# Hashed attention and a gated projection on one core: the seams between the stages are rewritten

## Chip, cores and metric

One NeuronCore of a Trainium2 chip runs the whole program in one launch. The metric is the device time of one execution in microseconds (us), the median of several runs. Before the change it is 904.46 us (3 runs, 904.19 to 904.78). The engines are TensorE (PE; its weight loads are shown as PEld), VectorE (DVE), ScalarE (ACT), GpSimd (POOL) and SyncE (SP); SP, ACT and POOL issue DMA transfers.

## The reference

```python
q_bits = (einsum('bhsd,dk->bhsk', q, proj) > 0)          # B,H,S,D = 4,8,768,64; 6 bits
k_bits = (einsum('bhsd,dk->bhsk', k, proj) > 0)
mask   = bucket(q_bits)[:, :, :, None] == bucket(k_bits)[:, :, None, :]
scores = where(mask, q @ k.T / sqrt(D), -1e9)
attn   = softmax(scores);  x = (attn @ v).reshape(B*S, H*D)   # 3072 x 512
h      = x @ w_in                                        # 512 x 2048
g      = h * erf(softplus(h))
out    = g @ w_out                                       # 3072 x 512, float32
```

A query attends only to keys whose six hash bits are the same as its own.

## The kernel before

**Attention.** The 32 heads are taken as 16 pairs; a pair fills the 128 partitions with two heads of 64. `fetch` loads q, k and v of a pair. Until now it issues one DMA for each head of the pair. For pair 0 (`quick`) q and k come in halves, and the first half of k goes by ACT's queue while everything else goes by SP's.

The hash bits of a pair become a second, bf16 operand of the score: a tile `both` with rows that add a huge amount when all bits agree, so that the exponential of a pair that does not agree is 0. Pair 0 and pair 1 make it directly (`hash_bits` with `proj_sb`, 64 columns for a head pair; then Sign on ACT, two weighings and a doubling on DVE: `place_first`, `weigh_first`, `double_first`). From pair 2 on it takes the shorter matmul with `proj_q` (line 845, 32 columns, four in the array at once), Sign (`sign_of`), one weighing (`weigh_bits`), and a way through DRAM that puts the rows in place: `leave_bits` writes them out and `place_bits` reads them back, both on POOL's DMA queue, into a `both` tile that was cleared (`clean`).

A pair has 4 score steps of 3 blocks each (line 557), then 4 weigh steps (line 642). PSUM holds three score blocks. `divisor` (line 687) sums the exponentials over the keys with a matmul against ones, and the reciprocal takes a way over DRAM (`spread`, `gather`, `invert`, `ungather`, `widen`).

Before all that, `WARM` matmuls on a tile of ones (line 807) run while the first loads are on their way. proj is loaded once into `proj_in` on POOL's queue and copied by DVE into `proj_sb` and `proj_q`.

**Bound.** The exponential is taken without a maximum. `measure` collects the squares of q and k; `judge` sums them over the partitions on PE (line 1746) and DVE takes the maxima, the product and the comparison, into `flag`. At the end of the program every engine loads `flag` (line 1776), and if the bound does not hold the general version runs (`tc.If`). With these inputs it does not run.

**Feed-forward.** Both products run as Strassen-like seven-product forms: P1 to P7 (line 1248) and M1 to M7 (line 1361), 24 blocks in all. `combine` makes the outputs of one tile of 512 tokens from the M banks and sends them; of the last tile, step 0 is a copy on ACT, steps 1 to 6 are whole additions on DVE, and steps 7 and 8 add the two halves of bank M3 and send each by ACT's queue.

**Order.** Each engine runs its instructions in written order. That order comes from a planner (`arrange`) that is given for each operation an engine, a guessed cost, what it comes after, and a rank; it runs its own clock and takes the operation that can start first, and between those that can start together the one of lower rank. For operations of rank 0 that are not on PE, a start within `PATIENCE` (0.16) of the first counts as together. An operation is written (its instructions are emitted) in the planner's order. Waits between engines are put in automatically from what each instruction reads and writes, in the order in which it was written.

PE's order in attention is a fixed chain: 4 scores, 4 weighs, then the next bits and the divisor; the bits of pair 1 come after the 4 scores of pair 0. Weight pieces (`fetch_weights`) are issued on POOL from the third on, each after the conversion (`add_rest`) of the third one before it.

Of the kernel before, what the change touches and what calls it, by code (L numbers as in the profile page):

```python
# [54 lines left out]
F32 = mybir.dt.float32  # L55
# [8 lines left out]
P = 128  # L64
# [132 lines left out]
def kernel(  # L197
# [35 lines left out]
    QR = 32  # L233
    QB = QR // 2
    WARM = 10
# [52 lines left out]
    nc.vector.memset(proj_q, 0.0)  # L288
    for ab in range(2):
        rows = slice(ab * D, ab * D + D)  # L290
        nc.vector.tensor_copy(
            out=proj_q[rows, ab * QB : ab * QB + NBIT],
            in_=proj_in[rows, ab * NBIT : (ab + 1) * NBIT],
        )
# [55 lines left out]
    def fetch(i, load, quick=False):  # L350
        d = dict(
            q=load.tile([P, S], F32, name="q", tag="q"),
            k=load.tile([P, S], F32, name="k", tag="k"),
            v=load.tile([P, NC, P], F32, name="v", tag="v"),
        )
        b, j = divmod(i, JP)
        parts = ((0, "q"), (0, "k"), (1, "k"), (1, "q")) if quick else ((None, "q"), (None, "k"))
        for half, what in parts:
            cols = slice(0, S) if half is None else slice(half * HS, half * HS + HS)
            queue = nc.scalar if quick and what == "k" and half == 0 else nc.sync  # L360
            for ab in range(2):
# [58 lines left out]
    def attention():  # L420
        NS = NPAIR * 4
        with (
# [18 lines left out]
            nc.vector.memset(e_even[:, :, :, HS : HS + 1], 1.0)  # L441
            e_odd = area[:, 0 : NE * S].rearrange("p (n a c) -> p n a c", n=NE, a=2)
# [279 lines left out]
            def spread(i):  # L722

                d = pairs[i]
                zd = d["zd"] = dram.tile([2, 4, HS // 2], F32, name="zd", tag="zd")
                d["zc"] = small.tile([P, 2 * S // P], F32, name="zc", tag="zc")
                nc.sync.dma_start(
                    out=zd.rearrange("h n c -> n h c"),
                    in_=d["z"][0 : 3 * QR + 1 : QR, 0:HS].rearrange("n (h c) -> n h c", h=2),
                )  # L730

            def gather(i):
                d = pairs[i]
                nc.sync.dma_start(
                    out=d["zc"],
                    in_=d.pop("zd")
                    .rearrange("h n c -> (h n c)")
                    .rearrange("(p c) -> p c", c=2 * S // P),
                )
# [64 lines left out]
            pairs[0] = fetch(0, load, quick=True)  # L804
            warm = bank("warm")
# [84 lines left out]
            def place_first():  # L890

                cols = slice(0, S)
                sign_bits(pairs[1], lambda what: both[1][:, "qk".index(what[0]), :], cols)

            def weigh_first(ab):
                spread_bits(pairs[1], slice(0, S), ab)

            def double_first():
                double_bits(pairs[1], slice(0, S))

# [19 lines left out]
            for what, n in order:  # L920
                free = slots[-3] if len(slots) >= 3 else ()
                if what == "score":
                    i = n // 4
                    after = (("double_first",) if i == 1 else ("place_bits", i),)
# [4 lines left out]
                elif what == "bits":  # L929
                    pe(bits_of, (n,), 0.80 if n > 1 else 1.44, (("start_pair", n),) + free)  # L930
                    slots.append((("sign_of", n),) if n > 1 else (("place_first",),))
# [54 lines left out]
            for i in range(NPAIR):  # L986
                n = 4 * i
                if i:
# [4 lines left out]
                        3.6,  # L993
# [3 lines left out]
                        late=3.5,  # L997
                    )
                    if i == 1:
                        op(place_first, (), "ACT", 0.9, (0, n - 2, 9), (("bits_of", i),))  # L1000
                        for ab in (1, 0):
                            op(weigh_first, (ab,), "DVE", 0.43, (0, n - 2, 1), (("place_first",),))
                        op(double_first, (), "DVE", 0.35, (0, n - 2, 2), (("weigh_first", 0), ("weigh_first", 1)))
                    else:
                        op(sign_of, (i,), "ACT", 0.6, (0, n - 6, 9), (("bits_of", i), ("leave_bits", i - 1)))
                        op(weigh_bits, (i,), "DVE", 0.33, (0, n - 6, 1), (("sign_of", i),))
                        op(leave_bits, (i,), "POOL", 0.7, (0, n - 6, 2), (("weigh_bits", i),), late=4.0, far=True)
                        op(
                            place_bits,
                            (i,),  # L1010
                            "POOL",
                            1.2,
                            (0, n - 6, 3),
                            (("leave_bits", i), ("score", n - 5, 2), ("clean", i - 2)),
                            late=3.6,
                        )
# [27 lines left out]
            for n in range(2):  # L1044
                op(clean, (n,), "POOL", 1.4, (0, 4 * n), (("score", 4 * n + 3, 2),), late=0.3)
# [155 lines left out]
    def feed_forward(check, late):  # L1201
        again = late is None
        with (
# [503 lines left out]
            if late:  # L1707
# [33 lines left out]
    def judge():  # L1741

        ps = bank("bound")[:, 0 : 4 * NPAIR]
        for ab in range(2):
# [7 lines left out]
            )  # L1752
        for ab in range(2):
# [5 lines left out]
            )  # L1759
        both = norms[:, :, 0, :]  # L1760
# [11 lines left out]

    with tc.manual_schedule():
        late = attention()
        feed_forward(judge, late)
    again = nc.values_load(flag[0:1, 0:1], min_val=0, max_val=1)
    with tc.If(again > 0):
# [55 lines left out]
```

## Time and profile before

| | |
|---|---|
| median of 3 runs | 904.46 us |
| the profiled execution, its time | 904.72 us |
| its span, first to last instruction | 902.9 us |
| PE busy | 894.3 us (99%) |
| DVE, ACT, POOL busy | 668.5, 563.3, 57.9 us |
| first matmul (warm) | 0.99 us |
| first hash matmul | 5.31 us |
| start of the scores of pair 1 | 27.33 us |
| first product of the feed-forward | 313.5 us |
| end of the last matmul | 896.2 us |

The span is what the profiler saw between the first and the last instruction; the execution's own time is 1.8 us longer. A row of the chain of waits is: start, duration, engine, tile, line, count. A row of the timeline is: start, duration, engine, line, operation, output<-inputs, shape, count, and in brackets how long the engine stood idle before it and what ended that. "SPq", "ACTq" are instructions of an engine's sequencer, DMA issues among them. A row of DMA issues is: output<-input, issuing engine, count, KB of each, and the median time from issue to landing. A matmul on float32 appears as two records.

### The profile page before, as it was taken

The page shows a single profiled execution, that of the slowest core. Times are in us where ns is not written, and L with a number is a line of the kernel's source. Part 1 is how long each engine was busy: PE and PEld are TensorE (multiplying, and loading weights), DVE is VectorE, ACT ScalarE, POOL GpSimd, SP SyncE. Part 2 cuts the span into 40 slices and gives each one's busy share as a digit, 9 for nine tenths or more (in the row PEclk, how much of TensorE's full clock was granted, in tenths as well). Part 3 has the DMA queues.
Part 4 walks back from the last instruction along what each step waited for, and adds up shares of the span by engine and source line. Part 5 has one row for each costly group of instructions (what it writes and reads, how often), then busy time and mean ns, then how long its engine had stood idle before and what let it go on. Part 6 is the DMA issues. An engine that isn't in the chain of part 4 may idle for free.

```text
span 902.9 us, 12780 instructions
## 1 busy us (share of the span) xinstructions
PE 894.3 (99%) x5016; PEld 670.9 (74%) x5016; DVE 668.5 (74%) x837; ACT 563.3 (62%) x808; POOL 57.9 (6%) x95
## 2 busy tenths in 40 slices
PE   9999999999999999999999999999999999999997
PEld 5455554455544588888888888888888888888886
DVE  5999999999999879995666556666776666655652
ACT  6788888788886668855645455545655555545520
POOL 1211211111110000000000001000100010000000
PEclk9999999999999999999999999999999999999999
DMA  9547655667551322202231013211421122111211
GB/s 228 149 128 183 200 166 142 196 173 195 154 157 60 101 89 65 82 36 70 59 106 58 14 49 103 82 36 47 105 83 36 36 74 78 35 36 57 63 68 50
DMA packets 65156, 86.82 MB, mean 96 GB/s; under 512 B 34364, under 2 KB 47772, under 8 KB 65088
## 3 DMA queue, kind: packets, MB, share of 16 engines
q1 hardware_dynamic: 56528, 63.81, 24.8%
q0 software_dynamic: 8112, 21.66, 8.6%
q8 instruction: 41, 0.67, 0.3%
q10 hardware_dynamic: 448, 0.46, 0.2%
q14 instruction: 27, 0.22, 0.1%
HBM read 64.67 MB, written 17.30 MB: 91 GB/s over the span
## 4 chain that ended last, share of the span: by engine, by line
PE 99%; DVE 0%; issue 0%; ACT 0%; DVEq 0%
PE M L1361 32%; PE X L1248 29%; PE st L557 17%; PE av L642 14%; PE M L1248 3%; PE bits L845 1%; PE bits L687 1%; PE warm L807 0%; PE bits L377 0%; PE z_ps L687 0%; DVE e L1288 0%; DVE h L1270 0%; ACT both L390 0%; DVE u L1396 0%; DVE norms L1754 0%
## 5 line engine op out<-in xcount | busy, mean ns | idle before, releaser
L1288 DVE SCALAR_TENSOR_TENSOR e<-w,e 128x1024 f32<-128x1024 f32 x144 | 173.7, 1220 | 8.4 <-ACT w L1282 3.9
L1248 PE MATMUL X<-area,w_in_sb 128*128 128x256 f32 x680 | 160.6, 379 | 0.0
L1282 ACT ACTIVATE w<-h,cq 128x1024 f32<-128x1024 f32 x144 | 155.6, 1136 | 0.1
L557 PE MATMUL st<-q,k 64*128 64x384 f32 x768 | 155.1, 482 | 0.0
L1270 DVE TENSOR_TENSOR h<-X,h 128x512 f32<-128x512 f32 x65 | 44.8, 689 | 144.4 <-PE X L1248 144.4
L1248 PEld LDWEIGHTS X<-area,w_in_sb 128*128 128x128 f32 x680 | 129.2, 190 | 17.6
L1361 PE MATMUL M<-w_out_sb,h 128*128 128x256 f32 x576 | 141.1, 379 | 0.0
L1248 PE MATMUL X<-area 128*128 128x256 f32 x520 | 122.8, 379 | 0.0
L1361 PEld LDWEIGHTS M<-w_out_sb,h 128*128 128x128 f32 x576 | 109.4, 190 | 14.9
L1266 ACT COPY h<-X 128x512 f32<-128x512 f32 x85 | 49.3, 580 | 111.4 <-PE X L1248 111.3
L1248 PEld LDWEIGHTS X<-area 128*128 128x128 f32 x520 | 98.8, 190 | 13.4
L1278 ACT ACTIVATE e<-h,cq 128x1024 f32<-128x1024 f32 x48 | 55.1, 1148 | 85.9 <-DVE h L1270 85.8
L1361 PE MATMUL M<-wt,S 128*128 128x256 f32 x384 | 95.1, 379 | 0.0
L557 PEld LDWEIGHTS st<-q,k 64*128 64x128 f32 x768 | 68.8, 187 | 29.7 <-issue 27.2
L630 DVE TENSOR_TENSOR area<-area 128x1536 f32<-128x1536 f32 (+1 forms) x46 | 79.2, 1723 | 7.5 <-ACT area L584 6.3
L1361 PEld LDWEIGHTS M<-wt,S 128*128 128x128 f32 x384 | 73.0, 190 | 9.9
L584 ACT ACTIVATE e_even<-st 128x768 f32<-128x768 f32 x96 | 70.6, 822 | 0.4 <-PE st L557 0.3
L584 ACT ACTIVATE area<-st 128x768 f32<-128x768 f32 x90 | 68.0, 817 | 0.0
L642 PE MATMUL av<-e_even,v 128*64 128x385 f32 x384 | 65.6, 490 | 0.0
L557 PE MATMUL st<-both 64*128 64x384 bf16 x384 | 63.5, 323 | 0.3 <-ACT both L390 0.3
L1303 DVE TENSOR_TENSOR h<-h,e 128x1024 f32<-128x1024 f32 x48 | 57.9, 1220 | 4.6 <-ACT e L1299 4.6
L642 PE MATMUL av<-area,v 128*64 128x384 f32 x360 | 60.6, 486 | 0.0
(129 smaller groups left out, 976.8 us busy)
## 6 DMA issues: line engine op xcount, KB each, us to landing
wt<-wt SPq DMA_DIRECT2D x24, 768.0 KB, 4.2
raw<-in_w_out_dram POOLq DMA_DIRECT2D x16, 512.0 KB, 4.2
raw<-in_w_in_dram POOLq DMA_DIRECT2D x14, 512.0 KB, 4.6
v<-in_v_dram SPq DMA_DIRECT2D x32, 192.0 KB, 4.6
q<-in_qkT_dram SPq DMA_DIRECT2D x30, 192.0 KB, 4.2
k<-in_qkT_dram SPq DMA_DIRECT2D x30, 192.0 KB, 4.7
r<-rd SPq DMA_DIRECT2D x30, 192.0 KB, 3.7
xs<-x SPq DMA_DIRECT2D x15, 384.0 KB, 3.0
```

The source lines that it names most:

```text
L557: nc.tensor.matmul(out=st[:, ab, 0:HS], lhsT=d["k" + src][rows, keys], rhs=d["q" + src][rows, cols], start=(part == 0), stop=(part == 1),)
L584: nc.scalar.activation(out=e[:, :, 0:HS], in_=st[:, :, 0:HS], func=AF.Exp, scale=scale)
L630: nc.vector.tensor_tensor(out=into, in0=one, in1=two, op=ALU.add)
L642: nc.tensor.matmul(out=d["av", half][rows, 0:w], lhsT=d["v"][:, g * GC + c, rows], rhs=e[:, ab, 0:w], start=(g == 0 and c == 0), stop=(g = ...
L1248: nc.tensor.matmul(out=d[where][:, u, :], lhsT=a[:, kc, f : f + P], rhs=b[:, kc, :], start=(first and u == 0 and kc == 0), stop=(last and ...
L1266: nc.scalar.copy(out=quarter(p, q), in_=st[p][where])
L1270: nc.vector.tensor_tensor(out=h, in0=st[p][where], in1=h, op=ALU.add)
L1278: nc.scalar.activation(out=s, in_=unit(p, v), func=AF.Sigmoid, bias=cq[:, n : n + 1])
L1282: nc.scalar.activation(out=q, in_=unit(p, v), func=AF.Sigmoid, scale=GATE_S[j][0], bias=cq[:, j : j + 1])
L1288: nc.vector.scalar_tensor_tensor(out=s, in0=st[p].pop(("q", v, j)), scalar=GATE_S[j][2], in1=s, op0=ALU.add, op1=ALU.mult,)
L1303: nc.vector.tensor_tensor(out=h, in0=h, in1=st[p].pop(("s", v)), op=ALU.mult)
L1361: nc.tensor.matmul(out=banks[name][:, sub, :], lhsT=a[:, u, sub * P : (sub + 1) * P], rhs=b[:, u, :], start=(c == 0 and k == 0), stop=(c = ...
```

## The change

- `fetch` issues one DMA for both heads of q and one for both of k; v stays two. proj is loaded twice without a copy by DVE: `proj_sb` on ACT's queue after the first k, `proj_q` on POOL's queue after the row numbers. `WARM` is 7 instead of 10.
- Pair 1 makes its hash bits the way of the later pairs (short matmul, Sign, one weighing, `leave_bits`, `place_bits`). Its matmul moves from behind the four scores of pair 0 to behind the second of them. `both[1]` is cleared once by DVE at the start, and only `both[0]` by POOL. The planner's cost and delay of `start_pair(1)` become 0.5 and 1.6 instead of 3.6 and 3.5.
- `divisor` does four matmuls of 384 columns instead of eight of 192; `spread` writes four rows.
- The check of the bound is cut into four: `measured` (the matmuls), `judge` (two reductions on DVE), `decide` (the four small operations that end in `flag`, of low rank, so wherever DVE is idle), and `ask` (every engine loads `flag`), written just before step 0 of the last `combine`.
- The last two matmuls of M3 of the last block are held back and written after step 7 of the last `combine`, ahead of step 8.

```diff
-    WARM = 10
+    WARM = 7
...
-    proj_in = const.tile([P, 2 * NBIT], F32, name="proj_in")
-    nc.gpsimd.dma_start(out=proj_in, in_=proj2)
     nc.vector.memset(proj_sb, 0.0)
-    for ab in range(2):
-        rows = slice(ab * D, ab * D + D)
-        nc.vector.tensor_copy(
-            out=proj_sb[rows, ab * QR : ab * QR + NBIT],
-            in_=proj_in[rows, ab * NBIT : (ab + 1) * NBIT],
-        )
+    nc.vector.memset(proj_q, 0.0)
+
+    def load_proj(queue, into):
+
+        queue.dma_start(
+            out=into[:, :].rearrange("p (a n) -> p a n", a=2)[:, :, 0:NBIT],
+            in_=proj2.rearrange("p (a n) -> p a n", a=2),
         )
+
     row = const.tile([P, 1], F32, name="row")
     nc.gpsimd.dma_start(out=row, in_=bucket)
+    load_proj(nc.gpsimd, proj_q)
...
-            for ab in range(2):
-                queue.dma_start(
-                    out=d[what][ab * D : ab * D + D, cols],
-                    in_=qkT[2 * i + ab, "qk".index(what) * D : "qk".index(what) * D + D, cols],
-                )
+            at = "qk".index(what) * D
+            queue.dma_start(
+                out=d[what][:, cols],
+                in_=qkT[2 * i : 2 * i + 2, at : at + D, cols],
+            )
...
             nc.vector.memset(e_even[:, :, :, HS : HS + 1], 1.0)
+            nc.vector.memset(both[1], 0.0)
...
-                for half in range(2):
-                    for n in range(4):
-                        ab, part = divmod(n, 2)
-                        nc.tensor.matmul(
-                            out=z[n * QR : (n + 1) * QR, half * HS // 2 : (half + 1) * HS // 2],
-                            lhsT=ones[:, 0:QR],
-                            rhs=d["sum"][:, half, ab, part * HS // 2 : (part + 1) * HS // 2],
-                            start=True,
-                            stop=True,
-                        )
+                for n in range(4):
+                    half, ab = divmod(n, 2)
+                    nc.tensor.matmul(
+                        out=z[n * QR : (n + 1) * QR, :],
+                        lhsT=ones[:, 0:QR],
+                        rhs=d["sum"][:, half, ab, :],
+                        start=True,
+                        stop=True,
+                    )
...
             pairs[0] = fetch(0, load, quick=True)
+            load_proj(nc.scalar, proj_sb)
...
-                if i == 1:
-                    hash_bits(pairs[i], big)
-                    return
                 d = pairs[i]
...
             for i in range(NPAIR):
-                order += [("score", 4 * i + k) for k in range(4)]
-                if i == 0:
-                    order.append(("bits", 1))
+                for k in range(4):
+                    order.append(("score", 4 * i + k))
+                    if i == 0 and k == 1:
+                        order.append(("bits", 1))
...
-                    after = (("double_first",) if i == 1 else ("place_bits", i),)
+                    after = (("place_bits", i),)
...
-                        3.6,
+                        3.6 if i > 1 else 0.5,
...
-                        late=3.5,
-                    )
+                        late=3.5 if i > 1 else 1.6,
+                    )
...
-            for n in range(2):
-                op(clean, (n,), "POOL", 1.4, (0, 4 * n), (("score", 4 * n + 3, 2),), late=0.3)
+            op(clean, (0,), "POOL", 1.4, (0, 0), (("score", 3, 2),), late=0.3)
...
-                op(("check", 0), "PE", 0.3, (0, 1, 9), check, (), after=(("P3", 0), ("late", 0)), late=1.5)
+                op(("check", 0), "PE", 0.2, (0, 1, 9), check[0], (), after=(("P3", 0), ("late", 0)))
+                op(("check", 1), "DVE", 0.4, (0, 1, 9.5), check[1], (), after=(("check", 0),))
+                op(("check", 2), "DVE", 0.6, (2, 8, 0), check[2], (), after=(("check", 1),))
                 for each in ops:
                     if each.name == ("P2", FILL - 1):
-                        each.after += (("check", 0),)
+                        each.after += (("check", 1),)
...
+            held = {("M3", NP - 1, f): None for f in (2, 3)}
             for each in arrange(ops, dict(h=8, e=4, w=4, wt=2), PATIENCE):
+                if check and each.name == ("combine", NTILE - 1, 0):
+                    check[3]()
+                if each.name in held:
+                    held[each.name] = each
+                    continue
                 each.emit()
+                if each.name == ("combine", NTILE - 1, 7):
+                    for other in held.values():
+                        other.emit()
...
+    def ask():
+
+        bound["again"] = nc.values_load(flag[0:1, 0:1], min_val=0, max_val=1)
+
     with tc.manual_schedule():
         late = attention()
-        feed_forward(judge, late)
-    again = nc.values_load(flag[0:1, 0:1], min_val=0, max_val=1)
-    with tc.If(again > 0):
+        feed_forward((measured, judge, decide, ask), late)
+    with tc.If(bound["again"] > 0):
```

More of the change, by code (lines that the diff above doesn't have):

```diff
@@ L287 @@
     nc.vector.reduce_sum(out=weight[:, 1:2], in_=steps[:, 2:5], axis=AX.X)
-    nc.vector.memset(proj_q, 0.0)
-    for ab in range(2):
[L290 to L293, printed above, removed]
-        )
     nc.vector.reduce_sum(out=weight_q, in_=steps[:, 5:8], axis=AX.X)
@@ L360, in fetch @@
             queue = nc.scalar if quick and what == "k" and half == 0 else nc.sync
-            for ab in range(2):
-                queue.dma_start(
-                    out=d[what][ab * D : ab * D + D, cols],
-                    in_=qkT[2 * i + ab, "qk".index(what) * D : "qk".index(what) * D + D, cols],
-                )
+            at = "qk".index(what) * D
[3 more added lines that the diff above has]
+            )
         for ab in range(2):
@@ L724, in spread @@
                 d = pairs[i]
-                zd = d["zd"] = dram.tile([2, 4, HS // 2], F32, name="zd", tag="zd")
+                zd = d["zd"] = dram.tile([4, HS], F32, name="zd", tag="zd")
                 d["zc"] = small.tile([P, 2 * S // P], F32, name="zc", tag="zc")
-                nc.sync.dma_start(
-                    out=zd.rearrange("h n c -> n h c"),
-                    in_=d["z"][0 : 3 * QR + 1 : QR, 0:HS].rearrange("n (h c) -> n h c", h=2),
-                )
+                nc.sync.dma_start(out=zd, in_=d["z"][0 : 3 * QR + 1 : QR, 0:HS])
             def gather(i):
@@ L736, in gather @@
                     in_=d.pop("zd")
-                    .rearrange("h n c -> (h n c)")
+                    .rearrange("n c -> (n c)")
                     .rearrange("(p c) -> p c", c=2 * S // P),
@@ L888, in place_bits @@
                     )
[L890 to L899, printed above, removed]
             def clean(n):
@@ L929, in attention @@
                 elif what == "bits":
-                    pe(bits_of, (n,), 0.80 if n > 1 else 1.44, (("start_pair", n),) + free)
-                    slots.append((("sign_of", n),) if n > 1 else (("place_first",),))
+                    pe(bits_of, (n,), 0.80, (("start_pair", n),) + free)
+                    slots.append((("sign_of", n),))
                 elif what == "divisor":
@@ L996, in attention @@
                         + tuple(("measure", i - 3, m, half) for m in range(2) for half in range(2)),
-                        late=3.5,
+                        late=3.5 if i > 1 else 1.6,
                     )
[L999 to L1016, printed above, removed]
+                    op(sign_of, (i,), "ACT", 0.6, (0, n - 6, 9), (("bits_of", i), ("leave_bits", i - 1)))
+                    op(weigh_bits, (i,), "DVE", 0.33, (0, n - 6, 1), (("sign_of", i),))
+                    op(leave_bits, (i,), "POOL", 0.7, (0, n - 6, 2), (("weigh_bits", i),), late=4.0, far=True)
+                    op(
+                        place_bits,
+                        (i,),
+                        "POOL",
+                        1.2,
+                        (0, n - 6, 3),
+                        (("leave_bits", i), ("score", n - 5, 2), ("clean", i - 2)),
+                        late=3.6,
+                    )
                 for m in range(2):
@@ L1739, with measured @@
     top = const.tile([1, 1], F32, name="top")
-    def judge():
-        ps = bank("bound")[:, 0 : 4 * NPAIR]
+    bound = {}
+    def measured():
+        ps = bound["ps"] = bank("bound")[:, 0 : 4 * NPAIR]
         for ab in range(2):
@@ L1752, in judge @@
             )
+    def judge():
+        ps = bound["ps"]
         for ab in range(2):
@@ L1759, in judge, with decide @@
             )
+    def decide():
         both = norms[:, :, 0, :]
```

## The prediction

> **What bounds the kernel now.** I read the page first (sections 1 and 4), then the chain of waits over 0–30, 330–345 and 890–903 us, then the timeline, the waits and the DMA issues at those places.
>
> ```profile
> span 902.9 us, 12780 instructions
> PE 894.3 (99%) x5016; PEld 670.9 (74%) x5016; DVE 668.5 (74%) x837; ACT 563.3 (62%) x808; POOL 57.9 (6%) x95
> PE 99%; DVE 0%; issue 0%; ACT 0%; DVEq 0%
> ```
>
> TensorE is the bound. 902.9 - 894.3 leaves 8.6 us without a matmul: 0.99 before the first, 6.69 after the last (ends 896.21), some 0.9 between. So this change can only shorten the seams, or take matmuls away. The chain of waits at the start:
>
> ```profile
> 0.99 4.49 PE warm L807 x20
> 5.48 0.70 PE bits L377 x4
> 9.17 8.25 PE st L557 x60
> 17.42 1.44 PE bits L377 x8
> 18.86 7.75 PE av L642 x48
> 26.62 0.78 PE bits L845 x8
> ```
>
> The warm matmuls are filler (10 calls, two records each). The pair-1 hash at line 377 costs 1.44; the other form, line 845, 0.78. The one mid-kernel stall:
>
> ```profile
> 333.71 0.23 PE bound L1746 x4
> 333.96 0.21 DVE norms L1754
> ...
> 334.44 0.19 DVE norms L1761
> 334.65 0.18 DVE top L1762
> 334.86 0.15 DVE top L1763
> 335.04 0.14 DVE flag L1771
> 335.18 0.72 DVE e L1288
> ...
> 337.48 0.70 DVE h L1270
> 338.22 3.72 PE M L1248 x16
> ```
>
> The chain leaves PE, runs through the six judging instructions, two multiplies and a completion on DVE, and returns to PE. The last two, and the next rows, are the tail and the loads:
>
> ```profile
> 896.24 0.76 DVE L1396 TENSOR_TENSOR u<-M,u 128x256 f32<-128x256 f32 x2 [0.44 <-PE M L1361]
> 896.69 1.84 ACTq L1405 DMA_DIRECT2D out_dram<-u  x2
> L1776 ACTq TENSOR_LOAD <-flag x1: 474/474/474, 898.6 to 898.6; - x1
> raw<-in_w_in_dram SPq DMA_DIRECT2D x2, 512.0 KB, 8.5
> bd<-sg POOLq DMA_DIRECT2D x14, 96.0 KB, 3.7
> both<-bd POOLq DMA_DIRECT2D x28, 21.0 KB, 2.5
> ```
>
> **The change, part by part.** The sum is made against the profiled execution, 904.72 us (span 902.9 and 1.8 around it); the median of the runs, 904.46, lies 0.26 lower and takes the same sum.
>
> *Start.* First hash matmul now: 5.31. It waits on two things that end together: the warm matmuls (20 records, 0.2135 apart, last at 5.10) and the second half of k, which the trace shows landed at 5.22 (issued 1.36, after the first head's). Seven warm calls end 6 x 0.2135 = 1.28 earlier, so the warm limit is 4.03 to 4.24. One transfer for both heads puts all of k and q on their queues at 0.75 instead of half of each at 1.36 and 1.40; the first halves landed 2.6 and 3.0 after issue, so twice the bytes should land by 3.8 to 4.4. proj goes from POOL (issued 1.30, landed 4.28, then two copies, "4.38 0.34 DVE L259") straight into proj_sb on ACT's queue behind k, issue about 1.3; latencies at the start were 2.6 to 3.9, so 4.0 to 5.2. Likely start 4.5, that is 0.8 earlier. But the PE ran at half rate until 5.31: 0.2135 per 128 columns in the warm matmuls, against 1.34 / 4 = 0.335 per 384 columns (0.112 per 128) in the later hash. If full rate comes at the same moment, the 0.8 us gained are done at half rate and only about 0.4 is won. I take 0.45; ends: 1.07 (4.24, full rate) and -0.3 (proj at 5.5). The row load now leads POOL's queue and the weights follow it by 1.1, ready by 5.9 before spread_bits needs them; the new memset of both[1] lies in DVE's idle 3.22 us before 4.38.
>
> [...]
>
> *Hash of pair 1.* Line 377's eight records took 17.35 to 18.69 = 1.34; line 845's eight take 0.67 before another 32-column matmul, 0.785 before a score (26.55 to 27.33). Gain 0.56 to 0.67; I take 0.6. Removed from ACT 0.90, from DVE 0.42 + 0.42 + 0.35; added 0.58 and 0.32, off the path. Its inputs: k of pair 1 landed at 12.48 before and goes out earlier now; the hash now stands after six score groups, about 12.0. Cover is thin there, about a microsecond.
>
> *The detour through DRAM.* Added on POOL: one leave (0.57 to issue), two place issues (0.58 each). The next pair's first score needs them. When? The scores of pair 1 began at 27.33; minus 0.45 and 0.6, 26.2. The hash ends at 12.7, Sign follows exp(1,2) on ACT, ends 13.5; weigh_bits comes behind the second sum on DVE (before: 13.82 to 15.58, now 0.45 earlier), ends 15.4; leave is issued at 15.5. On POOL's queue then stand clean(0) (before 16.90 + 1.38, now about 0.3 later), the third weight piece (issued before at 18.2), then place; the planner's costs in the code, used here for the order alone, put place (due 12.0) behind that piece (due 11) and well ahead of the fourth, which waits for add_rest(0) (planned about 18). leave at its 3.7, or 5 by my estimate for the load there, lands at 19 to 20.5, place issues until 21.5, plus 2.5 to 3.7: 24 to 25.5. Cover: some 1 us. Cost taken: 0; bounds 0 and 2.3 (both SP raw pieces there took 8.5; 8.5 for leave gives 24.0, place 25.2 issued, 28.2 to 28.5 landed). DMA is busy there (first slice of the page 9 tenths). If this cover is gone, each us late is a us of PE.
>
> *Divisor.* Eight matmuls of 192 columns in two rounds become four of 384. Rows: line 687 to the next score 0.766, line 845's like form 0.785. 15 x 0.02 = 0.3 lost at most; seen against the 0.67 that both take before another 32-column matmul, 0. I take 0.2 lost. One spread transfer of longer rows is off the path.
>
> *Judgement.* The last record before it started at 337.18 and takes 0.22, so PE waited 338.22 - 337.18 - 0.22 = 0.82 for the completion at 337.48. Lines 1761 to 1771 (334.44 to 335.11, the next multiply's start) leave this spot: 0.67 to 0.7 earlier. The two reductions stay before the multiply (their rank wins within the planner's patience: ready 20.09 against 19.97 + 0.16). 0.7 won; ends 0.3 (the four reappear in another tight place; DVE is 74% busy) and 0.82. Nothing else waits for the flag for 500 us.
>
> *Tail.* After 896.21: both last additions wait for the very last matmul, although the first reads only columns that the fourth record wrote (idle 0.44). So the ordering there goes by the whole bank. The change writes the first addition ahead of matmuls 2 and 3: it may start at 895.75 (after the sum w at 895.12 + 0.61) and end 896.17, but by the same ordering matmuls 2 and 3 then wait for it: 4 records from 896.25 (0.32 + 2 x 0.216 + 0.38), end 897.38, second addition until 897.83, its DMA issued at 897.93 instead of 897.09: 0.84 later. Against that: that DMA issue took 1.44 where the one before took 0.36; issues over 1.3 us coincide in this trace with an instruction fetch of PE, here at 896.9 after PE's branch. PE's branch now waits too, so the fetch falls near 897.5 and the issue should end near 898.8 (before 898.53). And the flag's load (0.47, with its gaps 0.55) no longer stands between this issue and ACT's branch at 899.12, which took 2.76 and ended the span's chain (SyncE waited 0.65 for it). Branch 898.85, so 0.3 won; ends +0.9 (short issue) and -0.5 (longer fetch). The loads on PE, DVE and ACT before the first combine run in idle time (ACT 21.34) or ahead of a filled PE queue (before: 892.17, four us early).
>
> **Sum:** 0.45 + 0.6 + 0 - 0.2 + 0.7 + 0.3 = 1.85. 904.72 - 1.85 = 902.87 profiled, 904.46 - 1.85 = 902.6 median: 0.2%, about what a measurement of this kernel can tell from no change.
>
> **Rivals.**
> (a) All seams pay: 1.07 + 0.67 + 0.82 + 0.9 = 3.5, time 901.0. For it: the warm limit of 4.24; against: proj behind k.
> (b) The bits of pair 1 are late by a congested leave: 28.4 - 26.2 = 2.2 lost, time 904.8. For: the 8.5; against: POOL's queue is another ring than SP's, the same transfers later take 3.7.
> (c) Slower: place_bits(1) is queued on POOL behind the fourth weight piece, which before was issued at 27.23 after waiting 8.47 us. Issues at 27.9 and 28.4, landing 30.9 to 31.5: 4.7 to 5.3 lost, time 907.5. It decides from a landing after 28.05 (all gains gone); over 0.2% slower from 29.9. For: the real clock has place ready near 20.5, far behind its due time of 12, and POOL runs in written order; against: by those due times place is written ahead by some 6 us.
> [...]
>
> **How the numbers follow.** Forecast 0.56, (a) 0.10, (b) 0.10, (c) 0.16, (d) 0.08. The forecast sits on the bound; the ends of its terms reach 901.4 to 903.9, two thirds of it I count as faster (the likely misses, a shorter issue at the end and an earlier clock, are gains): 0.36 faster, 0.20 same. Faster 0.36 + 0.10 = 0.46; same 0.20 + 0.10 + 0.08 = 0.38; slower 0.16. The range takes (a), (b), (d) and what lies between them and (c): 901.0 to 905.8; left out are (c) and the last of (a).
>
> **What would show it.** First hash matmul at 4.3 to 4.8; eight 845-records for pair 1 near 12; no PE wait on h L1270 near 337; first pair-1 score near 26.2 with no wait on both<-bd; PE idle near 1 us before the last four M records; no flag load after 890. Wrong if PE waits for POOL's DMA at 26, if warm-rate matmuls go on past 6, or if the span after the last matmul exceeds 6.7.

## The result, and the profile after

The changed kernel takes 1062.40 us (median of 6 runs, 1061.07 to 1063.54) against 904.62 us of the kernel before in the same session (904.18 to 905.03): 1.1744 times as long, 95% interval 1.1729 to 1.1759. The forecast of 902.6 us, its range to 905.8 and all its rivals, the slower one at 907.5 included, missed the event. The profiled execution took 1062.41 us with a span of 1060.5.

From the page of the kernel after: the span, PE's busy time, the granted PE clock by slice, the chain that ended last by engine, and two rows of its DMA issues.

```profile
span 1060.5 us, 12426 instructions
PE 941.1 (89%) x4882; PEld 679.0 (64%) x4882; DVE 667.7 (63%) x832; ACT 564.5 (53%) x808; POOL 58.5 (6%) x97
PEclk9789897989888888899999999999999999999999
PE 65%; DMA 14%; SPq 12%; DVE 3%; issue 3%; ACT 3%; POOL 0%; ACTq 0%; DVEq 0%; POOLq 0%
q<-in_qkT_dram SPq DMA_DIRECT2D x15, 384.0 KB
k<-in_qkT_dram SPq DMA_DIRECT2D x15, 384.0 KB
```

PE was the whole chain before; now a quarter of the chain is transfers and the queue that issues them. PE idles 119 us of the span, and it is busy 47 us longer than before with 134 instructions fewer. An estimated 35 of these 47 are the clock: by its records PE was busy 73.8 us at half rate, 4.3 before, and half of the difference is extra time; the other 12 are not accounted for here. The two DMA rows carry no time to landing, where before they had one (4.1 and 4.7 us in the same part of the span).

Next PE's waits, all of the span (engine, line waited at, releaser; total us, times, longest), and the start of PE's timeline.

```profile
PE bits L835 <- DMA k<-in_qkT_dram: 72.5, 14, 8.2
PE st L553 <- ACT z L693: 20.4, 9, 4.2
PE bits L372 <- DMA proj_sb<-in_proj_dram: 10.9, 1, 10.9
```
```profile
0.99 3.25 PE L800 MATMUL warm<-ones 128*64 128x128 f32 x14 [0.99 <-DVE ones L253]
15.17 0.87 PE L372 MATMUL bits<-q,proj_sb 128*64 128x384 f32 x1 [10.93 <-DMA proj_sb<-in_proj_dram]
```

The hash of almost every pair waits for k, and the first one stands at 15.17 us, 10 us after its place before. The feed-forward starts at 472.27 (before 313.46): 158.8 us later. From there to the end of the last matmul it takes 583.08 (before 582.74), and then 5.20 to the end of the span (before 6.66). So the whole loss lies in attention.

The chain of waits over the first 66 us shows how (start, us, what):

```profile
2.11 4.78 SPq L357
...
28.17 7.08 SPq L459
...
37.30 25.38 DMA k<-in_qkT_dram
62.68 0.04 issue
62.73 1.50 PE bits L835 x4
```

A load of k lands 25.38 us after its issue. SP's issues, 0.6 us in the median and 1.7 at most in attention before, take up to 7 us here (L459 is a piece of w_in) and up to 14.8 later, while the transfers ahead of them are still on their way; what holds them is not shown. What the transfer looks like on its way is seen in a stretch with almost nothing else under way: the DMA view over 128 to 132 us of the kernel after, and a loaded stretch of the kernel before, 105 to 109 us.

```profile
DMA packets 64, 0.20 MB, mean 51 GB/s; under 512 B 2, under 2 KB 2, under 8 KB 64
q1 hardware_dynamic: 49, 0.15, 9.5%
q0 software_dynamic: 15, 0.05, 3.3%
```
```profile
DMA packets 1135, 0.98 MB, mean 245 GB/s; under 512 B 885, under 2 KB 898, under 8 KB 1134
q1 hardware_dynamic: 1107, 0.89, 101.7%
```

The last column is packet time as a share of 16 engines. After: 9.5 + 3.3 = 12.8%, and 0.128 x 16 = 2.05 engines are at work, moving 51 GB/s. Before: all 16. The trace's semaphore updates agree: the merged load leaves 3 landings where a load of one head left 16 (q issued at 112.14: one at 113.16, then 124.76 and 124.90), and the destination in its issue reads [1,128] where one head's read [64,1]. Its source is the pattern [2 heads, 64 rows, columns].

### The profile page after: what moved, and what is told of

Same layout as the page of the kernel before. It is cut to its first block, busy times and chain, and to the rows that moved or that the text cites. A ratio compares the mean times of both kernels' runs of the same rounds, so it can differ in the third digit from the quotient of the medians.

```text
span 1060.5 us, 12426 instructions
## 1 busy us (share of the span) xinstructions
PE 941.1 (89%) x4882; PEld 679.0 (64%) x4882; DVE 667.7 (63%) x832; ACT 564.5 (53%) x808; POOL 58.5 (6%) x97
## 4 chain that ended last, share of the span: by engine, by line
PE 65%; DMA 14%; SPq 12%; DVE 3%; issue 3%; ACT 3%; POOL 0%; ACTq 0%; DVEq 0%; POOLq 0%
PE M L1334 27%; PE X L1221 24%; SPq L362 9%; PE st L553 8%; DMA k<-in_qkT_dram 7%; DMA zd<-z 4%; PE M L1221 3%; DVE area L626 2%; PE av L638 1%; DMA xs<-x 1%; SPq L357 1%; SPq L722 1%; DMA zc<-zd 1%; ACT e_even L580 1%; DMA raw<-in_w_out_dram 1%
## 5 line engine op out<-in xcount | busy, mean ns | idle before, releaser
L553 PE MATMUL st<-q,k 64*128 64x384 f32 x768 | 172.9, 531 | 0.0
L1239 ACT COPY h<-X 128x512 f32<-128x512 f32 x85 | 49.4, 581 | 112.3 <-PE X L1221 112.1
L553 PEld LDWEIGHTS st<-q,k 64*128 64x128 f32 x768 | 78.6, 210 | 33.6 <-issue 31.8
L553 PE MATMUL st<-both 64*128 64x384 bf16 x384 | 70.0, 353 | 22.2 <-ACT z L693 20.4
L736 DVE TENSOR_SCALAR zc<-zc 128x12 f32<-128x12 f32 x16 | 2.7, 168 | 129.5 <-DMA zc<-zd 129.5
L835 PE MATMUL bits<-k,proj_q 128*32 128x384 f32 x60 | 18.7, 713 | 72.5 <-DMA k<-in_qkT_dram 72.5
L703 ACT COPY x<-av 128x384 f32<-128x384 f32 x30 | 14.1, 474 | 127.1 <-DMA xs<-x 92.3
L553 PEld LDWEIGHTS <-both 64*128 64x128 bf16 x384 | 26.5, 101 | 76.1 <-issue 54.9
```

The source lines that it names most:

```text
L553: nc.tensor.matmul(out=st[:, ab, 0:HS], lhsT=d["k" + src][rows, keys], rhs=d["q" + src][rows, cols], start=(part == 0), stop=(part == 1),)
L835: nc.tensor.matmul(out=d["bits"][row : row + QR, 0, 0:HS], lhsT=proj_q, rhs=d[what][:, half * HS : (half + 1) * HS], start=True, stop=True,)
L1239: nc.scalar.copy(out=quarter(p, q), in_=st[p][where])
```

## The experiments

Theory T: the merged transfer runs on two DMA engines, as many as the outermost dimension of its source counts, and this alone is the loss. Its first rivals, C and S, are told in the expectations; K, L and N, on what is left of the loss at the start, come with the second group. All ratios are to the kernel before on the same chip.

**The merged loads alone.** The kernel before, with nothing but this:

```diff
-            for ab in range(2):
-                queue.dma_start(
-                    out=d[what][ab * D : ab * D + D, cols],
-                    in_=qkT[2 * i + ab, "qk".index(what) * D : "qk".index(what) * D + D, cols],
-                )
+            at = "qk".index(what) * D
+            queue.dma_start(out=d[what][:, cols], in_=qkT[2 * i : 2 * i + 2, at : at + D, cols])
```

> The kernel before with one edit: q and k of both heads in one transfer, source pattern [2, 64, columns]. Theory T (two engines): in the changed kernel each of these transfers counted 3 landings on its semaphore where every other load counted 16, and its issue row says dst_num_elem=[1,128] where the old one said [64,1]; so its rows run on 2 of the 16 DMA engines. 256 rows of 3072 B for a pair at 0.122 us a row are 16 us on each of two engines, and with their share of v and the weight pieces some 21 to 30 us for each pair where PE needs 19.2. Expected 1040 to 1080 us, attention ending near 470 instead of 313. Theory C (my rival: pair 1's bits held up on POOL): no change here, 904 to 905. Theory S (any 128-row issue is slow, engines aside): also slow here.

Measured: 1055.88 us (1054.43 to 1057.23), ratio 1.1668 [1.1650, 1.1686]. Its page:

```profile
span 1055.4 us, 12702 instructions
PE 64%; SPq 16%; DMA 13%; DVE 3%; ACT 2%; issue 1%; DVEq 0%; ACTq 0%
```

The same picture as after. One edit makes 151 of the 158 us.

**The change without the merged loads**: that edit undone in the changed kernel, two transfers again.

> The changed kernel with the old loads, one transfer for each head; everything else of the change is in. T: the loss is gone; what is left are the other seams, by my own terms 0.6 (hash) + 0.7 (judgement) + 0.3 (tail) - 0.2 (divisor) and little at the start, 902.6 to 903.6, no DMA wait of PE after 8 us. C: still slow, over 907. S: as T.

Measured: 905.97 us (903.72 to 906.90), ratio 1.0015 [1.0006, 1.0024]. T holds: the bytes and their places in memory are those of after, and the loss is gone. C falls: it said over 907, and PE has no wait on `both<-bd` in this trace. A second miss appears: the rest of the change, for which the forecast has a gain of 1.85 us, loses 1.4.

**One transfer, 128 rows.** As the change, one transfer for both heads, but q and k laid out in memory so that the two heads' rows follow each other and the source is [128, columns]:

```diff
-                in_=qkT[2 * i : 2 * i + 2, at : at + D, cols],
+                in_=qkT[i, "qk".index(what)][:, cols],
...
-    qkT = np.concatenate([q.transpose(0, 1, 3, 2), k.transpose(0, 1, 3, 2)], axis=2)
+    qkT = np.stack([w.transpose(0, 1, 3, 2).reshape(B * H // 2, 2 * D, S) for w in (q, k)], axis=1)
```

> The changed kernel, still one transfer for both heads, but the host lays the input out so that the 128 rows of a pair's q (and of its k) follow each other in DRAM and the source pattern is [128, columns]. T: 16 landings for each load, 902 to 903.5, first hash matmul at 4.3 to 5.0. S (the single 128-row transfer itself is slow): stays over 1000. C: over 907.

Measured: 906.16 us (904.55 to 907.37), ratio 1.0017 [1.0008, 1.0026], 16 landings a load. The same bytes in as many transfers and data packets as after: it is not the merging that costs, but the shape. S falls. The time is over the 902 to 903.5 that I expected, and the first hash stands at 6.32, not at 4.3 to 5.0: the second miss again.

**The kernel before with that layout and one transfer.**

> The kernel before with only that layout and one transfer of 128 rows. T: 903.8 to 904.6; ten warm matmuls hold the first hash at 5.1 to 5.3, so almost nothing can be won. S: over 1000.

Measured: 904.84 us (904.23 to 905.55), ratio 1.0002 [0.9993, 1.0011]. Done rightly, merging the loads alone is worth nothing here: PE was busy for 99% of the span before, so their time was hidden.

**An outermost dimension of 8, and of 4.** The change, with a layout whose source pattern is [8, 16, columns] or [4, 32, columns] (below for 8):

```diff
-                in_=qkT[2 * i : 2 * i + 2, at : at + D, cols],
+                in_=qkT[:, i, "qk".index(what)][:, :, cols],
...
+    qkT = np.stack([w.transpose(0, 1, 3, 2).reshape(B * H // 2, 8, 2 * D // 8, S) for w in (q, k)], axis=1)
+    qkT = qkT.transpose(2, 0, 1, 3, 4)
```

> The change with its merged loads, but q and k laid out in memory so that the transfer's outermost dimension is 8 and not 2. Theory T (a transfer runs on as many engines as its outermost dimension counts): 8 engines, 16 rows of 3072 B each at 0.13 us, 2.1 us a tensor where two engines took 9.8; the loop of SP's queue (loads, then the divisor's transfers behind them, 29.0 us a pair with two engines) falls below PE's 18.5 us a pair; only the start is a little later than with 16 engines: 906 to 909. If the landing is set by something other than the number of engines (the three-dimensional pattern itself), it stays near 1062.

> The same with an outermost dimension of 4. Theory T: 32 rows an engine, about 4.2 us a tensor; the loop of SP's queue takes 29.0 - 2 x (9.8 - 4.9) = 19.2 us or less a pair, at PE's own 18.5: from 908 (no loop limit, only a later start) to 918 (0.7 us in each of 15 pairs). The engines then count in proportion: 1062 at 2, at most 918 at 4, 909 at most at 8. If the pattern itself were the cause, near 1062.

Measured: 908.45 us (907.99 to 909.41), ratio 1.0050 [1.0036, 1.0065], with 8; 946.15 us (945.37 to 947.64), ratio 1.0461 [1.0446, 1.0476], with 4. Landings: 9 and 5. So an outermost dimension of 2, 4, 8 and 128, with 3, 5, 9 and 16 landings, gives 1062, 946, 908 and 906 us, and the three-dimensional pattern by itself costs at most the 2.3 us between the last two. For 2 the trace after shows 2.05 engines at work; that 4 and 8 run on as many is T's estimate from the landings. For 4 my figure (at most 918) was too low: the loop that I put at 19.2 us a pair takes 21.75 (22.3 in the mean of ten), seen in SP's queue of that run, from one load of q to the next:

```profile
123.25 0.58 SPq L356 DMA_DIRECT2D q<-in_qkT_dram  x1
...
139.09 0.34 SPq L725 DMA_DIRECT2D zc<-zd  x1
...
145.00 0.58 SPq L356 DMA_DIRECT2D q<-in_qkT_dram  x1
```

k there landed 14.4 us after q's issue, where the outermost 2 took 22.6: 8.2 saved, not the 9.8 of my halving, and the rest of the loop is 0.9 longer.

**Only the first pair merged**: the changed kernel, with the merged transfer under `if quick` and two transfers for all later pairs.

> The change with one transfer for both heads in the first pair alone and two transfers in all later pairs. Theory T in two parts: at the start two engines carry 128 rows of 1536 B a half tensor, first hash at about 15.2 and second at about 20.7 as in the whole change, against 6.5 and 10.9 with two transfers; from pair 1 on, no loop of 29 us a pair. So only 8 to 10 us of the 156 us between the whole change and the version with two transfers remain: 914 to 916, feed-forward from 325 to 327. If the late start itself, by pushing every later load back, caused the rest, the time is well over 920.

Measured: 921.18 us (920.77 to 921.55), ratio 1.0185 [1.0168, 1.0202], some 5 more than expected, and at the edge of the rival's "well over 920". Its chain at the start:

```profile
2.12 19.10 DMA q<-in_qkT_dram
21.22 0.14 issue
21.35 0.87 PE bits L379 x4
```

The feed-forward begins at 328.43, 11.5 us later than with two transfers everywhere (316.98); I had expected 8 to 10. The rest of the overshoot is 2.6 us behind the last matmul (7.56 against 4.93): the last transfer lands as early as there (3.19 and 3.07 after the last matmul), but ACT reaches the program's closing instructions 2.9 us later (6.59 against 3.72). Why is open. Of the 155.3 us by which the feed-forward starts later with the merged loads, the first pair alone thus makes 11.5, and 143.8 come with the later pairs.

**The start: 16 warm calls.** With two transfers, the change still has its first hash at 6.47 and the feed-forward at 316.98, 3.5 later than before. From here on the base is the changed kernel with two transfers. First edit: `WARM = 16` for 7.

> The change with the two old transfers a tensor, and 16 warm calls for 7. With seven, that kernel's PE idled from about 4.0 to 6.47 us (proj_sb landed at 6.33 on ACT's queue) and ran at half rate until 12.54; the feed-forward began at 316.98 us against 313.46 before. Theory K (the loss at the start is the clock, which stays at half rate because PE idles before the first hash): sixteen calls keep PE busy to 6 or past it, the clock is at full rate from about 6, the hash at 6.5 and all behind it runs at full rate: 6.07 us of half rate gone, 3.0 us won, feed-forward from 313.9, time 903.0. Theory L (the loss is only that proj lands late, and the clock would have come at 12.5 anyway): feed-forward from 317, time 906.0.

Measured: 904.23 us (903.72 to 904.76), ratio 0.9998 [0.9989, 1.0007]. The chains at the start, first with 7 calls, then with 16:

```profile
2.27 4.06 DMA proj_sb<-in_proj_dram
6.33 0.14 issue
6.47 1.64 PE bits L372 x4
8.11 2.86 PE st L553 x8
```
```profile
0.99 6.05 PE warm L800 x31
7.05 0.76 PE bits L372 x4
7.80 1.49 PE st L553 x8
```

Same matmuls, half the time: 1.64 and 2.86 against 0.76 and 1.49. With seven calls PE idles from 4.24 to 6.47 until proj arrives, and full rate came at 12.54; with sixteen it came at 6.03. The hash starts later (6.78 against 6.47) and yet the feed-forward begins 2.3 us earlier, at 314.66. K holds against L; I had expected 3.0; the later hash takes some of it back.

**The old way of proj, with 7 and with 10 warm calls.** proj once on POOL's queue ahead of the row numbers, and two copies by DVE, as before:

```diff
-            load_proj(nc.scalar, proj_sb)
...
+    proj_in = const.tile([P, 2 * NBIT], F32, name="proj_in")
+    nc.gpsimd.dma_start(out=proj_in, in_=proj2)
```

> The change with the two old transfers a tensor and the old way of proj (first on POOL's queue, two copies by DVE), seven warm calls. proj_sb should be ready at 4.7 to 5.2 us. Theory L (only the late proj costs): hash at 4.7 to 5.2, full rate soon after, feed-forward from 312.5 to 313, time 902.3 to 902.9. Theory K (idling shuts the clock): PE idles 0.7 to 1.2 us ahead of the hash; if that is enough to keep the clock at half rate for one more stretch of 3.4 us, 1.7 us is lost and the feed-forward begins at 314.4, time 904.4.

> As the one before, with ten warm calls: the start is that of the kernel before; what is left of the change is pair 1's short hash by way of DRAM, the divisor, the judgement in parts, the early flag and the held matmuls. Theories K and L alike: first hash at 5.2 to 5.5, clock full from there, first score of pair 1 about 0.56 earlier than before, feed-forward from 312.9 (313.46 - 0.56), feed-forward 583.1 long and 5.1 behind it as in the two runs seen, span 901.1, time 902.9: 1.5 us faster than before. If instead the parts other than the start win nothing (theory N), 904.4.

Measured with 7: 903.31 us (902.85 to 905.56), ratio 0.9993 [0.9984, 1.0002]. The eleven times lie in two groups, 902.9 to 903.8 and 905.0 to 905.6: near what L says and what K says. The profiled execution (904.95) is of the second: first hash at 5.20 after an idle stretch of 0.96 us, full rate only from 9.74, feed-forward from 315.08. With 10: 903.31 us (902.75 to 904.28), ratio 0.9987 [0.9978, 0.9996], some 1.2 us less than before, and the interval lies below 1; full rate from 5.14, feed-forward from 312.95. N falls: the other parts do gain.

**Without holding the two matmuls.** The run before with 10 calls, and the last two matmuls of M3 written in their place:

```diff
-                if each.name in held:
-                    held[each.name] = each
-                    continue
                 each.emit()
-                if each.name == ("combine", NTILE - 1, 7):
-                    for other in held.values():
-                        other.emit()
```

> As the one before, without holding the last two matmuls of M3. The hold made PE wait 1.01 us (1.23 between two starts, 0.22 of it the matmul itself) ahead of its last four records. My prediction's ordering (the addition waits for the whole bank): without it the feed-forward takes 582.07, and the tail grows from 5.1 to between 5.9 and 6.4 because the second addition and its transfer come later behind the last matmul, no flag load between: time within 0.3 of the run with the hold. Rival: the hold is worth its 0.9 in the tail whole, and this is 0.5 or more slower; or the tail does not depend on it (it is set by something else, an instruction fetch or the transfer's landing), and this is 0.8 to 1.0 faster.

Measured: 902.95 us (901.97 to 903.71), ratio 0.9981 [0.9972, 0.9990]. This is under both kernels, 1.5 us under the kernel before. The timeline of the run with the hold, and below it ACT's issue of the last two transfers without it:

```profile
894.90 1.13 PE L1338 MATMUL M<-w_out_sb,S 128*128 128x256 f32 x4 [0.85 <-DVE u L1373]
```
```profile
896.25 1.31 ACTq L1382 DMA_DIRECT2D out_dram<-u  x2
```

The held records wait for the addition that only reads the other half of their bank. The feed-forward is 1.12 shorter without them (581.96 against 583.08), the tail 0.54 longer (5.48 against 4.94). By these two traces the hold loses 0.6. But the tail differs from trace to trace: 4.79 to 5.27 us in eight traces with the hold and 7.56 in the ninth, and 6.58 in the other one without it (the next run), by which the hold would win 0.5. The two medians differ by 0.36, less than either run's spread. PE's 1.12 is shown; whether the hold pays or costs is open.

**The last one with rows that lie together and 8 warm calls.**

> The best of the last runs (old way of proj, no held matmuls, pair 1's short hash, divisor, judgement in parts, early flag: 902.95) with both heads of q and of k in one transfer of 128 rows that lie together in memory, and 8 warm calls. All of q and k lands by 4.4 us (seen: 4.39 and 4.51), proj_sb is copied at 4.4 to 5.2, so the first hash starts at 4.4 to 5.2 for 5.2, warm matmuls end at 4.4. [...] Rival: pair 1's rows come back from DRAM at 26.6 to 26.9 as in the last two runs, and with an earlier start its first score waits for them: 902.9 to 903.3.

Measured: 903.12 us (902.62 to 906.04), ratio 0.9987 [0.9979, 0.9996]. No better than the run before (902.95): all of k and the first half of q were there by 4.48, but proj_in landed at 4.69 (4.05 in the run before), so the first hash stood at 5.19 again. In the two traces the feed-forward starts 0.6 earlier (313.18 for 313.79, full rate from 5.85 for 7.11) and the tail is 1.1 longer; neither is tied to the edit by anything measured here. Pair 1's rows were back at 23.56, so the rival's wait was not the reason.

## Why the prediction was wrong

**The step that failed: "Start", "One transfer for both heads puts all of k and q on their queues at 0.75 ... twice the bytes should land by 3.8 to 4.4".** I counted bytes and issue times, and never asked over how many engines the new pattern spreads (2.05 at work in the trace after). There, the four halves landed at 10.70, 13.90, 16.45 and 20.60. The first hash waited for proj, which stood behind the first k on ACT's queue and landed at 15.04. Against the range, this one term was off by over 150 us.

The price could have been worked out from the trace of before. It has one transfer of this kind: the divisor's `zd<-z`, whose pattern starts with 4 rows, leaves 5 landings on its semaphore where the loads have 16, and among the DMA issues of 95 to 145 us it is the one row without a landing time. A packet of 3072 B occupies an engine there for 0.12 us at least and 0.14 in the median. Had I read those 5 landings as four engines, and so expected two for an outermost 2, my estimate for 128 rows would have been 64 x 0.12 to 0.14 = 7.7 to 9.0 us a tensor, and q and k of a pair at 15 to 18: nearly a whole pair's time on PE (18.5), so hardly any cover is left. Measured in the kernel after: 9.8 us from q's landing to k's. The landings here are 3, 5, 9 and 16 for an outermost 2, 4, 8 and 128: up to 8, one more than the dimension counts.

Why 29 us a pair and not 18.5: SP's queue closes a loop, here in the kernel after.

```profile
112.14 0.56 SPq L357 DMA_DIRECT2D q<-in_qkT_dram  x1
112.79 0.54 SPq L357 DMA_DIRECT2D k<-in_qkT_dram  x1
113.42 8.65 SPq L362 DMA_DIRECT2D v<-in_v_dram  x2
122.17 9.80 SPq L722 DMA_DIRECT2D zd<-z  x1
132.02 0.43 SPq L773 DMA_DIRECT2D xs<-x  x1
136.21 0.34 SPq L726 DMA_DIRECT2D zc<-zd  x1
138.36 0.32 SPq L744 DMA_DIRECT2D rd<-zc  x1
139.77 0.63 SPq L754 DMA_DIRECT2D r<-rd  x1
```

q lands at 124.90, k at 134.71; the last landings of v (136.01) and of the divisor's `zd` (136.19) come behind them; `zc`, `rd` and `r` follow one after the other on SP's queue, and the next pair's q is issued only behind them, at 141.15: 29.0 us after this one. The last ten such loops, from 112.1 to 408.3, average 29.6 us. 29.6 - 18.5 = 11.1 more a pair, 111 of the 143.8 us; the rest falls to the pairs before and behind them.

The waits for ACT's z at L553, 20.4 us, fit the same loop: ACT's copies into x wait for a transfer of that queue, as the group's row shows (last column: idle time before it, and what ended it). In the loop above `xs` lands at 136.97, ACT's copy into x starts at 137.07 after 9.4 us idle, its copy into z at 139.62, and PE's score at 140.14.

```profile
L703 ACT COPY x<-av 128x384 f32<-128x384 f32 x30 | 14.1, 474 | 127.1 <-DMA xs<-x 92.3
```

**The second failure, in the same step: proj "issue about 1.3 ... 4.0 to 5.2", and the 0.08 for (d).** Where q and k left 16 landings, proj on ACT's queue landed at 6.33 (two transfers ahead of it, issued 2.27) or 6.18 (one ahead, issued 1.20, 4.99 on the way). Seven warm calls end at 4.24. I had taken it that hash and scores follow the last warm call within 0.3 us; PE idled 2.2 and 2.1 us. By (d) I meant a clock that stays at half rate longer, at about 1.7 us lost: my estimate, which no run shows. In its place the runs showed full rate at 12.54 and 11.13 (in the second trace it had also been open from 4.30 to 7.72) where ten calls had it at 5.31, and 2.1 to 3.5 us lost by the start of the feed-forward. The sum has no term for this.

**The other terms**, from the run with the old start and the hold, whose first hash is at 5.24 (before 5.31), and the one without the hold:

| term | forecast | measured |
|---|---|---|
| hash of pair 1 | 0.6 | 0.40: second hash to pair 2's hash 18.55 us (before 18.95) |
| detour through DRAM | 0 | 0: no wait; rows back at 26.57, first score of pair 1 at 26.87 |
| divisor | -0.2 | +0.05: pair 2's hash to the feed-forward 286.86 (before 286.91) |
| judgement | 0.7 | 0.78: feed-forward 581.96 (before 582.74), unheld |
| tail, hold included | 0.3 | 0.60: 1.72 shorter, 1.12 of it given back on PE |

Mechanisms held, but for the long issue in the tail, and most sizes; the hash lies below its bounds (0.56 to 0.67). The hash of eight short matmuls takes the 0.785 that I used, which alone is a gain of 0.56; 0.10 of it is lost in pair 0's scores, which it now splits (9.05 us for 8.95), and 0.05 in the weigh steps (7.91 for 7.86):

```profile
12.52 0.78 PE bits L839 x8
```

The chain past the judgement no longer leaves PE (without the hold; compare the norms, top and flag rows of before):

```profile
329.93 4.10 PE M L1225 x19
334.03 0.21 PE bound L1729 x4
334.24 7.26 PE M L1225 x32
```

The detour's margin was thin as said, but for another reason: `leave_bits` took 6.72 us to land, not 3.7 to 5, and the rows still came 0.3 us ahead of the first score. That much was luck: the same transfer took 5.93 us in the run without the hold (0.9 us ahead), 2.84 in the change with two transfers and 2.32 in the last run (3.5 ahead in both). So (b)'s congestion came without its cost, and (c) did not come: POOL issued `place_bits` at 23.17, the fourth weight piece behind it at 26.58.

In the tail the orderings were right (the addition waits for the last matmul of its bank, 0.44 us idle without the hold, and the held matmuls for the addition, 0.85), and in these two traces the gain was larger than worked out. By the other traces (tails of 6.66 to 7.08 us with the flag load at the end, 4.79 to 5.27 with the hold, one of 7.56 left aside) it lies between 0.3 and 1.2. Without the hold, in that trace: no flag load (0.47) on ACT, the second issue 0.91 for 1.44, and 1.93 from the last landing to the end for 2.60. With it the last issue takes 0.34, not the 0.87 that I had from an instruction fetch beside it. A packet of an instruction queue (q8) is under way from 0.50 to 1.43 us after the last matmul there, with the issue at 0.49 to 0.83, so my reading that a long issue comes from such a fetch is not borne out.

Of the signs to look for, in the trace after, those on the hash's form (not its place), on the wait near 337, on PE's idling ahead of the last four records and on the flag came out as written; the first hash (15.17) did not, and neither did pair 1's first score. Of the signs of being wrong, warm-rate matmuls past 6 us came (full rate first at 19.24).

## What to carry to other kernels

Before two transfers become one, write down the outermost dimension of both sides' patterns: in these runs a source with an outermost 2, 4, 8 and 128 took 1062, 946, 908 and 906 us, and the price per byte of loads with 16 landings was not that of the first two. In the profile, a load with fewer than 16 landings (3, 5 and 9), or a stretch whose DMA share is 2 of 16 while everybody waits (12.8% over 128 to 132 us), was the sign; the cure here was a layout in which the partitions are one dimension (906.16 us). And filler matmuls belong up to the first real one: shortening them without bringing the data earlier moved the clock's opening back, from 6.03 to 12.54 between 16 calls and 7.

## What the runs showed that was not expected

- **PE's idle time and the granted clock.** In the trace after, the granted clock changes only at steps of 3.413 us. Stepping through it from the first opening (19.24 us), with PE's idle time in each step: the 15 steps at half rate that end with an opening have at most 0.31 us of idle time, and the 15 that end without one have 0.86 us or more. The clock stayed open over steps with up to 1.90 us, and the 15 closings before the last matmul come at the end of steps with 1.81 or more, as far as the modelled ends of the matmuls allow. These are one trace's counts; a bound is not shown. The two runs with ten calls and the old proj start alike and opened at 5.14 and 7.11, and the two groups of times with seven calls lie 2 us apart, though only one of those executions was traced; what decides it is not shown.
- **proj took longer to land as a strided load.** In runs of 24 bytes, 256 of them, it took 3.7 to 5.0 us on ACT's or POOL's queue where the loads beside it left 16 landings; one transfer of 48 bytes a row took 2.8 to 3.5, and DVE's copies 0.35 more. It was also issued later, behind other loads, and no run parts the two causes.
- **Other transfers landed later too.** In the kernel after, loads that left 16 landings took longer than before, those of POOL's queue too: raw pieces of w_in 7.5 us for 4.9, `both<-bd` 5.2 for 2.5 (both kernels over 100 to 300 us). Of the 16 landings of the second v issued behind q and k in the loop above, 14 came by 124.47 and the last two at 135.70 and 136.01.
